# Point products of an FFT stage: three fp32r products from split operands in place of one float32 product

## The chip, the core and the metric

The kernel runs on one core of a Trainium2 chip. The metric is the device time of one execution in microseconds; the median of three executions is compared. The engines of a core work side by side: TensorE (PE in the profile; PEld is its weight load), VectorE (DVE), ScalarE (ACT), GpSimd (POOL) and SyncE (SP), the last of which here only issues DMA transfers.

## The reference

Three stages, eight batches of 3072 positions with 256 channels:

```python
X = np.fft.rfft(x, axis=1)
Y = X * (filt_r + 1j * filt_i)[None]
x = np.fft.irfft(Y, n=3072, axis=1).reshape(8 * 3072, 256)

h = np.maximum(np.maximum(x @ w1, x @ w2), x @ w3)       # d_ff 768
x = h @ w_out

h = x @ w_in                                             # d_ff 1024
e = np.exp(h - h.max(-1)); solu = h * e / (e.sum(-1) + 1e-9)
ln = (solu - mean) / sqrt(var + 1e-6) * g_ln
out = ln @ w_out
```

All data are float32 (the MoE weights float64, split in the kernel).

## The kernel before

Each of the sixteen channel halves ("channels" below, two for each batch, 128 columns wide) goes through an FFT of 3072 = 24 x 128 points, a product with the filter and the inverse FFT. The 24-point part is sums on VectorE (`dft8`, `fwd3` forward, `inv3`, `idft8` back). The 128-point part is a product with constant matrices on TensorE, the point product (`prod`, line 440), for four groups g of frequencies:

- `fwd_in` forms the twiddled input U (six blocks of 128 columns for groups 0 to 2, four for group 3) with two scalings on ScalarE and sums on VectorE.
- `middle` multiplies U by the matrices MA0 and MA1 into a PSUM tile pf, folds the result (Z), exchanges the partition halves of Z by DMA (`swap`), multiplies by the filter F (M1, M2), subtracts and adds on GpSimd, exchanges again, and forms EO with two operations on VectorE.
- `inv_out` multiplies EO by MB0 and MB1 into pf, and ScalarE and VectorE apply the inverse twiddles into the channel's slab S.

Channels 0 and 1 (`ch < FULL`) go the same way with full complex matrices (`dfull`) in `first_batch`, ahead of the first MoE. Channels 2 to 15 run as a stream of Python generators (`fft_stream`). The main loop traces one MoE step (`moe`: 12 products of `up`, 6 of `down`, in fp32r high and low terms), and then draws from the stream until a share of VectorE work (RATE, 3200 ns by the kernel's own costs) is spent, or nothing was spent in twelve draws. `later()` makes a generator yield until the next step has been traced; `behind_step()` orders VectorE's sums behind a MoE operation. A batch has 36 steps; the loop covers seven batches (`n_a`), and the last batch runs beside the weights of the second MoE. A channel can start when its slab is free (`free`), and its result must be there when `have` asks for it, one tile of the MoE ahead; the planner then puts the traced instructions of each engine in one fixed order.

Where a tile tag has one buffer, the next use waits for the last reader of the one before. Before the change U and EO have two buffers each (pool `f2`), M2 and the swap tile one (pool `fc`), and pf is one tile of two banks (`pairbank`) which the forward and the inverse products of all channels share. Products of float32 operands are issued as two instructions each; those of fp32r operands as one.

Of the kernel before, what the change touches and what calls it, by code (L numbers as in the profile page):

```python
# [20 lines left out]
P = 128  # L21
# [124 lines left out]
def kernel(ctx: ExitStack, tc: tile.TileContext, x0, xr, ff, tw, dft, first_f, first_i,  # L146
# [136 lines left out]

    FULL = 2

    cost = [0.0]

    def tt(o, a, b, op, eng=nc.vector):
# [146 lines left out]
        return t[:, j0:j1].rearrange("p s d -> p (s d)")  # L435

    def prod(o, mat, src, i0=None, i1=None, first=True, last=True):
        m = df[:, mat] if mat < 7 else dfull[:, mat - 7]
        v = src if i0 is None else rows(src, i0, i1)
        FZ['mm'] = nc.tensor.matmul(o, m, v, start=first, stop=last).ins  # L440

    def fwd_in(ch, g):
        sl, ks = GROUPS[g]
        X = S[ch]
        U = f2.tile([P, 8, P], F32, tag="U", name="U")
        n = len(ks)
        T = fc.tile([P, 6, P], F32, tag="T", name="T")
        if sl:
            for j, k in enumerate(ks):
                nc.scalar.activation(T[:, j:j + 4:3], X[:, sl:sl + 2, j], AF.Copy, scale=col("s", k))  # L450
                nc.scalar.activation(U[:, j:j + 4:3], X[:, sl:sl + 2, j], AF.Copy, scale=col("c", k))
            yield
            tt(U[:, 0:3], U[:, 0:3], T[:, 3:6], ALU.add)
            yield
            tt(U[:, 3:6], U[:, 3:6], T[:, 0:3], ALU.subtract)
            yield
        elif ch >= FULL:
            t, d = X[:, :, 1], X[:, :, 2]
            for j, k in enumerate((8, 20)):
                nc.scalar.activation(T[:, j], d[:, j], AF.Copy, scale=col("sh", k))  # L460
                nc.scalar.activation(U[:, j], t[:, j], AF.Copy, scale=col("c", k))
                nc.scalar.activation(T[:, 2 + j], d[:, j], AF.Copy, scale=col("ch", k))
                nc.scalar.activation(U[:, 2 + j], t[:, j], AF.Copy, scale=col("ns", k))
            yield
            tt(U[:, 0:4], U[:, 0:4], T[:, 0:4], ALU.add)
            yield
        else:
            t, d = X[:, :, 1], X[:, :, 2]
            nc.scalar.copy(U[:, 0], X[:, 0, 0])
            nc.scalar.activation(U[:, 1], X[:, 1, 0], AF.Copy, scale=col("c", 12))  # L470
            nc.scalar.activation(U[:, 5], X[:, 1, 0], AF.Copy, scale=col("ns", 12))
            nc.gpsimd.memset(U[:, 4], 0.0)
            yield
            for j, k in enumerate((8, 20)):
                nc.scalar.activation(T[:, j], d[:, j], AF.Copy, scale=col("sh", k))
                nc.scalar.activation(U[:, 2 + j], t[:, j], AF.Copy, scale=col("c", k))
                nc.scalar.activation(T[:, 2 + j], d[:, j], AF.Copy, scale=col("ch", k))
                nc.scalar.activation(U[:, 6 + j], t[:, j], AF.Copy, scale=col("ns", k))
            yield
            uu = U.rearrange("p (r s) d -> p r s d", r=2)[:, :, 2:4]  # L480
            tt(uu, uu, T[:, 0:4].rearrange("p (r s) d -> p r s d", r=2), ALU.add)
            yield
        ST["u", ch, g] = U
        yield

# [13 lines left out]
    def middle(ch, g):  # L499
        dc = ch % 2  # L500
        sl, ks = GROUPS[g]
        n = len(ks)
        W = n * P
        real = g == 3 and ch >= FULL
        R = 2 * P if real else 0
        foff = sum(2 * P * len(GROUPS[i][1]) for i in range(4 if real else g))

        def pair(tag, name, pool=fc):
            t = pool.tile([P, 2, 4, P], F32, tag=tag, name=name)
            return t.rearrange("p r s d -> p (r s d)")[:, :2 * W].rearrange("p (r w) -> p r w", r=2)  # L510

        def swap(v):

            t = fc.tile([P, 512], F32, tag="swap", name="swap")[:, :v.free_size()]
            nc.sync.dma_start(t[64:], v[:64])
            nc.sync.dma_start(t[:64], v[64:])
            return t

        odd = ch < 2 and UNITS.index((ch, g)) % 2
        F = pair("Z" if odd else "F", "F")  # L520
        nc.sync.dma_start(F.rearrange("p r w -> p (r w)"), ff[dc, :, foff:foff + 2 * W])
        src = ST.pop(("u", ch, g))
        pf = pairbank(ch)
        if ch < FULL:
            for r, (mr, mi) in enumerate(((FRR, FIR), (FRI, FII))):
                prod(pf[:, r, :W], mr, src, 0, n, True, False)
                prod(pf[:, r, :W], mi, src, n, 2 * n, False, True)
                yield
            M1 = pair("EO", "Y", f2)
            M2 = pair("M2" if odd else "M1", "M2")  # L530
            tt(M1, pf[:, 0:1, :W].to_broadcast([P, 2, W]), F, ALU.mult)
            yield
            tt(M2, pf[:, 1:2, :W].to_broadcast([P, 2, W]), F, ALU.mult)
            yield
            tt(M1[:, 0], M1[:, 0], M2[:, 1], ALU.subtract)
            SUMS[ch, g] = tt(M1[:, 1], M1[:, 1], M2[:, 0], ALU.add).ins
            yield
            ST["y", ch, g] = M1
            yield
            return  # L540
        u = col("u", 0)
        if real:
            prod(pf[:, 0, 0:P], MO, S[ch][:, 1, 0])
            prod(pf[:, 0, P:R], MF0, S[ch][:, 0, 0])
            prod(pf[:, 0, R:W], MA0, src, 0, 2)
            yield
            prod(pf[:, 1, R:W], MA1, src, 2, 4)
            TAKEN.add(ch)
        else:
            prod(pf[:, 0, :W], MA0, src, 0, n)  # L550
            yield
            prod(pf[:, 1, :W], MA1, src, n, 2 * n)
        yield
        Z = pair("Z", "Z")
        M2 = pair("M2", "M2")
        nc.scalar.mul(M2[:, 0, R:], pf[:, 1, R:W], -1.0)
        nc.scalar.copy(M2[:, 1, R:], pf[:, 0, R:W])
        if real:
            nc.scalar.copy(Z[:, 0, :R], pf[:, 0, :R])
        stt(Z[:, :, R:], pf[:, :, R:W], u, M2[:, :, R:])  # L560
        ZS = swap(Z[:, 0])
        yield
        M1 = pair("M1", "M1")
        tt(M1[:, :, R:], Z[:, 1:2, R:].to_broadcast([P, 2, W - R]), F[:, :, R:], ALU.mult)
        if real:
            tt(M1[:, 0, :R], Z[:, 0, :R], F[:, 0, :R], ALU.mult)
        yield
        EO = pair("EO", "EO", f2)
        tt(M2[:, :, R:], ZS[:, R:].unsqueeze(1).to_broadcast([P, 2, W - R]), F[:, :, R:], ALU.mult)
        if real:  # L570
            stt(M2[:, 1, :R], ZS[:, :R], col("sg", 0), F[:, 1, :R], ALU.mult)
        yield
        tt(M1[:, 1, R:], M1[:, 1, R:], M2[:, 0, R:], ALU.subtract, nc.gpsimd)
        RS = swap(M1[:, 1, R:])
        tt(M1[:, 0, R:], M1[:, 0, R:], M2[:, 1, R:], ALU.add, nc.gpsimd)
        if real:
            tt(EO[:, 0, :R], M1[:, 0, :R], M2[:, 1, :R], ALU.add, nc.gpsimd)
        yield
        yield from later()
        with behind_step():  # L580
            stt(EO[:, 0, R:], RS, u, M1[:, 0, R:], ALU.subtract)
            stt(EO[:, 1, R:], M1[:, 0, R:], u, RS)
        yield
        ST["y", ch, g] = EO
        yield

    def inv_out(ch, g):
# [3 lines left out]
        io = 0 if sl else 1  # L591
        src = ST.pop(("y", ch, g))
        pf = pairbank(ch)
        src = src.rearrange("p r (s d) -> p (r s) d", d=P)
        if ch < FULL:
            prod(pf[:, 0, :W], IRR, src, 0, n, True, False)
            prod(pf[:, 0, :W], IIR, src, n, 2 * n, False, True)
            yield
            prod(pf[:, 1, io * P:W], IRI, src, io, n, True, False)
            prod(pf[:, 1, io * P:W], III, src, n + io, 2 * n, False, True)  # L600
        elif not sl:
            prod(pf[:, 0, :P], MOI, src, 0, 1)
            prod(pf[:, 0, P:W], MB0, src, 1, n)
            yield
            prod(pf[:, 1, 2 * P:W], MB1, src, n + 2, 2 * n)
        else:
            prod(pf[:, 0, :W], MB0, src, 0, n)
            yield
            prod(pf[:, 1, io * P:W], MB1, src, n + io, 2 * n)
        yield  # L610

        def zz(r, j):
# [146 lines left out]
    def first_batch():  # L759
# [6 lines left out]
        xa = []  # L766
        for ch in range(2):
            xa.append(((fc if ch else yp).tile([P, 24, P], F32, tag=f"s{ch + 2}", name="xa"),
                       f2.tile([P, 8, P], F32, tag="EO", name="xq")))
            for q in range(4):  # L770
                nc.sync.dma_start(xa[ch][0][:NT, 8 * q:8 * q + 8] if q < 3 else xa[ch][1][:NT],
                                  x0[ch, :, 8 * q:8 * q + 8])
# [40 lines left out]
        for i, u in enumerate(UNITS):  # L813
# [28 lines left out]
            if i == 7:  # L842
                turn_in(0, 0, *UNITS[6])
        GATE.append(behind)
        with tc.issue_after(FZ["mm"]), tc.issue_after(FZ["sent"].ins):
            for q in range(4):
                quarter(3, q, nc.scalar, xs[3, q])
            busy(3)
# [477 lines left out]
```

## Time and profile before

| | |
|---|---|
| median of three executions | 2670.12 us (2669.33 to 2671.59) |
| profiled execution | 2671.45 us |
| its span, first to last instruction | 2669.7 us |
| TensorE busy | 2649.1 us (99%), granted clock 0.999 in the mean |
| weight loads busy | 2180.8 us (82%) |
| VectorE | 2114.0 us (79%) |
| ScalarE | 1559.3 us (58%) |
| GpSimd | 893.8 us (33%) |
| transfers from GpSimd's queue (the software ring) | 1296 packets, 4.72 MB |
| chain that ended last | 65% on TensorE, 2% of the span at the point products |

Busy times are the union of an engine's instructions. TensorE's instructions overlap, so the duration of one is longer than the distance from its start to the next start; when one is followed by another without a wait, that distance is its price. The FFT beside the first MoE lies between about 97 and 1340 us of the span, and the second MoE fills the rest from about 1600 us.

### The profile page before, as it was taken

What the parts mean: (1) busy time and instruction counts of PE and PEld (TensorE: products, weight loads), DVE (VectorE), ACT (ScalarE), POOL (GpSimd) and SP (SyncE); (2) the same over time, 40 slices, a digit from 0 to 9 for tenths busy, and PEclk for the clock granted to TensorE, in tenths of its full rate; (3) what the DMA queues carried; (4) which work ended last, traced back from release to release, by engine and by line L of the source; (5) the groups of instructions that cost most, each with busy time, mean ns of one, the idle gap of its engine ahead of it and who ended that gap; (6) DMA issues with size and microseconds to landing.
All of it is one profiled execution on the core that took longest, in us unless ns stands there. A gap on an engine that the chain in (4) does not pass through costs nothing.

```text
span 2669.7 us, 38591 instructions
## 1 busy us (share of the span) xinstructions
PE 2649.1 (99%) x12458; PEld 2180.8 (82%) x12458; DVE 2114.0 (79%) x3545; ACT 1559.3 (58%) x2960; POOL 893.8 (33%) x1311
## 2 busy tenths in 40 slices
PE   8999999999999999999999999999999999999999
PEld 5778888877887888888788888888888888888888
DVE  6887788988988988988785448878888878787875
ACT  5645554454454554554543336777777777777775
POOL 0011121011010010010110005666667676767675
PEclk9999999999999999999999999999999999999999
DMA  8534222224133242232222105555555555555543
GB/s 246 153 110 133 84 80 75 83 74 129 49 86 110 64 121 69 69 95 62 81 85 80 42 22 138 149 139 147 146 142 143 143 146 141 142 145 149 139 129 87
DMA packets 169063, 295.56 MB, mean 111 GB/s; under 512 B 33724, under 2 KB 101052, under 8 KB 167228
## 3 DMA queue, kind: packets, MB, share of 16 engines
q1 hardware_dynamic: 113848, 231.49, 32.4%
q10 hardware_dynamic: 53716, 56.89, 6.6%
q0 software_dynamic: 1296, 4.72, 0.6%
q8 instruction: 98, 1.61, 0.3%
q14 instruction: 105, 0.86, 0.1%
HBM read 97.40 MB, written 56.62 MB: 58 GB/s over the span
## 4 chain that ended last, share of the span: by engine, by line
PE 65%; DVE 2%; DMA 1%; SPq 1%; issue 1%; ACT 0%; POOL 0%; DVEq 0%; ACTq 0%; POOLq 0%
PE h L1112 20%; PE h L921 14%; PE p L1181 13%; PE p L1183 7%; PE o L942 2%; PE o L943 2%; PE o L941 2%; PE o L950 2%; PE pf L440 2%; SPq L881 1%; DMA raw<-in_w_out_dram 0%; DVE scr L291 0%; DMA raw<-in_w_in_dram 0%; DVE h L926 0%; DVE hl L930 0%
## 5 line engine op out<-in xcount | busy, mean ns | idle before, releaser
L291 POOL TENSOR_TENSOR M<-M,M 128x384 f32<-128x384 f32 (+1 forms) x112 | 129.8, 1179 | 1088.2 <-DVE M L291 921.2
L1174 POOL TENSOR_TENSOR sl<-zt,sh 128x1024 fp32r<-128x1024 f32 x188 | 453.4, 2412 | 120.9 <-ACT sh L1173 111.5
L929 ACT CAST hh<-h 128x512 fp32r<-128x512 f32 x288 | 169.3, 589 | 378.3 <-DVE h L926 369.2
L1181 PE MATMUL p<-V,sh 128*128 128x512 f32 x1536 | 380.4, 389 | 0.0
L1123 DVE SCALAR_TENSOR_TENSOR sp<-h,e 128x1024 f32<-128x1024 f32 x192 | 234.1, 1220 | 153.5 <-ACT e L1121 151.4
L1181 PEld LDWEIGHTS p<-V,sh 128*128 128x128 f32 x1536 | 287.3, 188 | 59.3
L1121 ACT ACTIVATE e<-h,sm 128x1024 f32<-128x1024 f32 x192 | 213.8, 1114 | 111.9 <-DVE sm L1119 68.3
L924 ACT ACTIVATE hm<-h 128x512 f32<-128x512 f32 x288 | 174.2, 606 | 170.5 <-PE h L921 169.5
L1119 DVE TENSOR_REDUCE sm<-h 128x1 f32<-128x1024 f32 x192 | 231.6, 1206 | 46.4 <-PE h L1112 45.3
L1173 ACT CAST sh<-zt 128x1024 fp32r<-128x1024 f32 x188 | 196.5, 1046 | 106.5 <-PE p L1181 92.6
L1125 ACT ACTIVATE e<-sp,sm 128x1024 f32<-128x1024 f32 x192 | 220.5, 1148 | 54.1 <-DVE sm L1127 46.8
L1112 PE MATMUL h<-wih,x2h 128*128 128x512 f32 x768 | 243.1, 392 | 1.2 <-ACT xo L953 1.2
L1112 PE MATMUL h<-wih,x2l 128*128 128x512 f32 x768 | 242.0, 391 | 0.0
L926 DVE TENSOR_TENSOR h<-hm,h 128x512 f32<-128x512 f32 x288 | 198.2, 690 | 51.2 <-PE h L921 46.8
L1112 PE MATMUL h<-wil,x2h 128*128 128x512 f32 x768 | 238.3, 390 | 0.0
L1140 DVE STREAM_TRANSPOSE yt<-sp 128x1024 f32<-128x1024 f32 x188 | 231.5, 1231 | 4.4 <-issue 0.5
L930 DVE TENSOR_TENSOR hl<-h,hh 128x512 fp32r<-128x512 f32 x288 | 197.2, 686 | 45.8 <-ACT hh L929 45.2
L941 PE MATMUL o<-hh,woh 128*128 128x512 f32 x576 | 232.6, 404 | 0.0
L942 PE MATMUL o<-hl,woh 128*128 128x512 f32 x576 | 228.1, 396 | 0.3 <-DVE hl L930 0.3
L943 PE MATMUL o<-hh,wol 128*128 128x512 f32 x576 | 225.8, 392 | 0.0
L1183 PEld LDWEIGHTS p<-V,sl 128*128 128x128 f32 x1536 | 209.7, 190 | 15.0
L1183 PE MATMUL p<-V,sl 128*128 128x256 f32 x1536 | 214.9, 282 | 0.0
(185 smaller groups left out, 5622.4 us busy)
## 6 DMA issues: line engine op xcount, KB each, us to landing
zt<-yt SPq DMA_DIRECT2D x752, 128.0 KB
x<-xo SPq DMA_DIRECT2D x96, 256.0 KB
x<-x ACTq DMA_DIRECT2D x48, 512.0 KB
F<-in_ff_dram SPq DMA_DIRECT2D x48, 384.0 KB
S<-in_xr_dram SPq DMA_DIRECT2D x12, 1536.0 KB
out_dram<-ob ACTq DMA_DIRECT2D x144, 128.0 KB
zt<-yt SPq DMA_DIRECT2D x560, 32.0 KB
F<-in_ff_dram SPq DMA_DIRECT2D x16, 512.0 KB
```

The costliest lines, as they stand in the source:

```text
L921: nc.tensor.matmul(ph[j], wt[:, c, f * P:(f + 1) * P], xt[:, c], start=i == 0, stop=i == 5)
L941: nc.tensor.matmul(po[m], wo_h[:, f, cs], hh, start=f == 0, stop=False)
L942: nc.tensor.matmul(po[m], wo_h[:, f, cs], hl, start=False, stop=False)
L943: nc.tensor.matmul(po[m], wo_l[:, f, cs], hh, start=False, stop=False)
L1112: nc.tensor.matmul(h[:, fs], xt[:, c, ts], wt[:, c, fs], start=n == 0, stop=n == 5)
L1119: nc.vector.tensor_reduce(sm[:, 0:1], h, axis=AX.X, op=ALU.max, negate=True)
L1123: nc.vector.scalar_tensor_tensor(sp, h, 1.0, e, op0=ALU.mult, op1=ALU.mult, accum_out=sm[:, 2:3])
L1125: nc.scalar.activation(e, sp, AF.Square, bias=sm[:, 3:4], accum_out=sm[:, 4:5])
L1140: nc.vector.transpose(out=YT[g][:, :, t].rearrange("p j c k -> p c j k"), in_=sp.rearrange("p (c j k) -> p c j k", c=NF2, j=4))
L1174: nc.gpsimd.tensor_tensor(lv, z, hv, op=ALU.subtract)
L1181: nc.tensor.matmul(p, sh[:, c], V2[:, c], start=c == 0, stop=False)
L1183: nc.tensor.matmul(p[:, :D], sl[:, c], V2[:, c, :D], start=False, stop=c == NF2 - 1)
```

## The change

- For channels 2 to 15 a new helper `split` rounds an operand to fp32r on ScalarE (hi) and subtracts hi from the operand on GpSimd (lo, also fp32r). `fwd_in` splits U of every group after its sums, `middle` splits EO of groups 0 to 2; both yield `later()` first, so the split is traced behind the next MoE step.
- `prod` with a split operand issues three fp32r products into the same PSUM range: high matrix with hi, low matrix with hi, high matrix with lo. The high and low matrices of MA0, MA1, MB0 and MB1 are formed once, after the first two channels, in the place of `dfull`. Group 3's EO and the two products MO and MF0 with slab columns stay float32.
- Buffers: U and EO have one buffer, with a hi tile and a lo tile beside it; the first two channels alternate between the operand's tile and the hi tile. M2 and the swap tile have two buffers. The inverse product of MB1 takes the whole width without `io`, which is 0 there.
- The scratch for dynamic DMA descriptors is set to 4096 bytes.

```diff
+    def split(v, tag, n):
+        hi = fc.tile([P, 8, P], F32R, tag=tag + "2", name=tag + "h")[:, :n]
+        lo = fc.tile([P, 6, P], F32R, tag=tag + "l", name=tag + "l")[:, :n]
+        nc.scalar.copy(hi, v)
+        nc.gpsimd.tensor_tensor(lo, v, hi, op=ALU.subtract)
+        return hi, lo
...
     def prod(o, mat, src, i0=None, i1=None, first=True, last=True):
+        if isinstance(src, tuple):
+            hi, lo = (rows(v, i0, i1) for v in src)
+            dh, dl = FZ["dh"][:, mat], FZ["dl"][:, mat]
+            nc.tensor.matmul(o, dh, hi, start=True, stop=False)
+            nc.tensor.matmul(o, dl, hi, start=False, stop=False)
+            nc.tensor.matmul(o, dh, lo, start=False, stop=True)
+            return
...
-        U = f2.tile([P, 8, P], F32, tag="U", name="U")
+        odd = ch < 2 and UNITS.index((ch, g)) % 2
+        U = fc.tile([P, 8, P], F32, tag="U2" if odd else "U", name="U")
...
+        if ch >= FULL:
+            yield from later()
+            U = split(U[:, :2 * n] if sl else U[:, :4], "U", 2 * n if sl else 4)
         ST["u", ch, g] = U
...
-            t = fc.tile([P, 512], F32, tag="swap", name="swap")[:, :v.free_size()]
+            t = f2.tile([P, 512], F32, tag="swap", name="swap")[:, :v.free_size()]
...
-            M1 = pair("EO", "Y", f2)
-            M2 = pair("M2" if odd else "M1", "M2")
+            M1 = pair("EO2" if odd else "EO", "Y")
+            M2 = pair("M2", "M2", f2)
...
-        M2 = pair("M2", "M2")
+        M2 = pair("M2", "M2", f2)
...
-        EO = pair("EO", "EO", f2)
+        EO = pair("EO", "EO")
...
+        if sl:
+            yield from later()
+            EO = split(EO.rearrange("p r (s d) -> p (r s) d", d=P), "EO", 6)
         ST["y", ch, g] = EO
...
-            prod(pf[:, 1, io * P:W], MB1, src, n + io, 2 * n)
+            prod(pf[:, 1, :W], MB1, src, n, 2 * n)
...
+        dd = fc.tile([P, 2, 4, P], F32R, tag="dfull", name="dd")
+        FZ["dh"], FZ["dl"] = dd[:, 0], dd[:, 1]
+        with tc.issue_after(FZ["sent"].ins):
+            nc.scalar.copy(FZ["dh"], df[:, 0:4])
+        nc.gpsimd.tensor_tensor(FZ["dl"], df[:, 0:4], FZ["dh"], op=ALU.subtract)
...
-    nc = bacc.Bacc("TRN2", target_bir_lowering=False, num_devices=1)
+    nc = bacc.Bacc("TRN2", target_bir_lowering=False, num_devices=1, dynamic_dma_scratch_size=4096)
```

## Rows read from the trace of the kernel before

**Rows 1.** Busy time by stretch: TensorE, weight loads, VectorE, ScalarE, GpSimd; clock, DMA.
```profile
97.00:1340.00 1243.00, 1239.00 (x5488) 999.05 (x5487) 1064.06 (x1639) 643.00 (x1462) 143.01 (x127) 1.00 0.30 88
```
**Rows 2.** Waits of TensorE, 97 to 1340 us: total, times, longest.
```profile
PE pf L440 <- POOL EO L291: 0.3, 1, 0.3
```
**Rows 3.** Order of time on TensorE, 1000.6 to 1002.7 us: start, duration, instructions.
```profile
1000.66 1.45 PE L440 MATMUL pf<-U,df 128*128 128x384 f32 x4
...
1002.18 0.63 PE L921 MATMUL h<-xh,w1h 128*128 128x512 f32 x2
```
**Rows 4.** Order of time on TensorE, 2000 to 2003 us, fp32r operands.
```profile
2000.19 1.98 PE L1181 MATMUL p<-V,sh 128*128 128x512 f32 x8
2002.01 1.12 PE L1183 MATMUL p<-V,sl 128*128 128x256 f32 x8
2002.96 0.40 PE L1112 MATMUL h<-wih,x2h 128*128 128x512 f32 x1
```
**Rows 5.** Order of time on TensorE, 1322 to 1324 us.
```profile
1322.43 1.03 PE L440 MATMUL pf<-U,df 128*128 128x256 f32 x4
...
1323.53 0.40 PE L942 MATMUL o<-hl,woh 128*128 128x512 f32 x1
```
**Rows 6.** Groups of TensorE by shape, point products: busy us, mean ns, idle before.
```profile
L440 PE MATMUL pf<-EO,df 128*128 128x384 f32 x196 | 72.6, 486 | 0.0
L440 PE MATMUL pf<-U,df 128*128 128x384 f32 x168 | 61.0, 485 | 0.0
...
L440 PE MATMUL pf<-U,df 128*128 128x256 f32 x56 | 14.4, 380 | 0.0
```
**Rows 7.** Groups by shape: a cast on ScalarE, a subtraction on GpSimd.
```profile
L1174 POOL TENSOR_TENSOR sl<-zt,sh 128x1024 fp32r<-128x1024 f32 x188 | 453.4, 2412 | 120.9 <-ACT sh L1173 111.5 <-PE p L1183 3.5 <-PE h L1112 2.4
...
L1173 ACT CAST sh<-zt 128x1024 fp32r<-128x1024 f32 x188 | 196.5, 1046 | 106.5 <-PE p L1181 92.6 <-POOL sm L1130 10.5 <-POOL sm L1131 2.1
```
**Rows 8.** Order of time on GpSimd, two places.
```profile
928.09 2.31 POOL L291 TENSOR_TENSOR M<-M,M 128x384 f32<-128x384 f32 x2 [11.94 <-DVE M L291]
...
1288.96 1.97 POOL L291 TENSOR_TENSOR M<-M,M 128x384 f32<-128x384 f32 x2 [66.17 <-ACT hm L924]
```
**Rows 9.** Order of time on VectorE, two places.
```profile
928.47 2.34 DVE L291 TENSOR_TENSOR S<-S,T 128x384 f32<-128x384 f32 x2
...
1319.20 1.02 DVE L291 TENSOR_TENSOR S<-S,T 128x384 f32<-128x384 f32 x2
```
**Rows 10.** Order of time on VectorE: the last sum of an operand.
```profile
511.49 1.02 DVE L291 TENSOR_TENSOR U<-U,T 128x384 f32<-128x384 f32 x2
...
1293.86 0.61 DVE L295 SCALAR_TENSOR_TENSOR EO<-M,tws,swap 128x384 f32<-128x384 f32 x1
...
1303.07 0.61 DVE L295 SCALAR_TENSOR_TENSOR EO<-M,tws,swap 128x384 f32<-128x384 f32 x1
```
**Rows 11.** Order of time on TensorE: the products of those operands.
```profile
513.04 1.45 PE L440 MATMUL pf<-U,df 128*128 128x384 f32 x4
...
1297.80 1.45 PE L440 MATMUL pf<-EO,df 128*128 128x384 f32 x4
...
1313.85 1.45 PE L440 MATMUL pf<-EO,df 128*128 128x384 f32 x4
```
**Rows 12.** Busy time by stretch of a pair (channels 13, 14), columns as rows 1.
```profile
1090.00:1163.00 73.00, 73.00 (x314) 58.20 (x313) 63.23 (x101) 43.08 (x104) 8.91 (x9) 1.00 0.29 79
1163.00:1229.00 66.00, 66.00 (x284) 52.60 (x283) 52.56 (x81) 31.09 (x71) 9.72 (x9) 1.00 0.37 106
1229.00:1281.00 52.00, 52.00 (x231) 43.07 (x230) 50.64 (x79) 25.55 (x55) 0.00 (x0) 1.00 0.14 40
```
**Rows 13.** Order of time on VectorE: the last operations of channel 15.
```profile
1358.52 1.82 DVE L295 SCALAR_TENSOR_TENSOR S<-scr 128x768 f32<-128x768 f32 x2
```
**Rows 14.** Order of time on TensorE: the first product of the last batch.
```profile
1430.05 0.62 PE L921 MATMUL h<-xh,w0h 128*128 128x512 f32 x2
```
**Rows 15.** The tile raws, 0 to 150 us: its transfers' time to landing.
```profile
DMA to landing us min/median/max: 4.1/4.9/11.2
```

More of the change, by code (lines that the diff above doesn't have):

```diff
@@ L593, in inv_out @@
         pf = pairbank(ch)
-        src = src.rearrange("p r (s d) -> p (r s) d", d=P)
+        if not isinstance(src, tuple):
+            src = src.rearrange("p r (s d) -> p (r s) d", d=P)
         if ch < FULL:
@@ L768, in first_batch @@
             xa.append(((fc if ch else yp).tile([P, 24, P], F32, tag=f"s{ch + 2}", name="xa"),
-                       f2.tile([P, 8, P], F32, tag="EO", name="xq")))
+                       fc.tile([P, 8, P], F32, tag="EO2" if ch else "EO", name="xq")))
             for q in range(4):
```

## The prediction

> **What bounds the kernel now.** I read the busy times first [rows 1]. From 97 us to 1340 us, where the FFT of channels 2 to 15 runs beside the first MoE, TensorE is busy for 1239.0 of 1243 us at a granted clock of 1.00, VectorE for 1064, ScalarE for 643, GpSimd for 143. So TensorE stands still for 4 us there, and the waits put 0.3 us of it at the point products, on the one operand that GpSimd makes today [rows 2]. This half is bound by TensorE's own work: a microsecond of it removed is a microsecond gained, unless a new wait takes its place. Behind 1340 us the change touches nothing, so all that it brings comes from the FFT half. The busy times of single groups overlap (a fp32r product shows 0.39 us and starts 0.23 us after the one before), so I take prices from starts alone.
>
> **The price of a float32 product.** A float32 product is issued as two instructions. In [rows 3] four of them (two products of 384 columns) start at 1000.66; with one fp32r product of 512 columns behind them they last until the next start at 1002.18. One fp32r product of 512 takes 0.2275 us: eight of them from 2000.19 to 2002.01 [rows 4]. So four instructions take 1.52 - 0.23 = 1.29 us, 0.322 each, 0.644 for a product. At 256 columns: 1322.43 to 1323.53 is 1.10 us [rows 5], less 0.23 is 0.87 for four, 0.435 for a product.
>
> **The price of its three fp32r products.** 256 columns: eight from 2002.01 to 2002.96 [rows 4], 0.119 each, three make 0.356. No row shows fp32r with 384 columns; its neighbours bound it, 0.119 (256) and 0.2275 (512), so three cost 0.356 to 0.683. The two prices lie on a line of 0.425 ns a column with 10 ns added, so I take 0.173, three 0.519. A product of 384 saves 0.644 - 0.519 = 0.125 us, one of 256 saves 0.435 - 0.356 = 0.079. The third weight load costs nothing: loads of 128 columns keep pace with products that start every 0.119 us too [rows 4].
>
> The Trainium skill, "TensorE: Matmul & The Clock Gate", Back-to-back issue gap, gives a sustained roofline of 81 ns a product at N=128 and 131 ns at N=512; an estimate between the two, about 114 ns at 384, would make three 0.34 us and the whole gain near 55 us. The trace differs: 227 ns at 512 in an unbroken stream, so the measurement decides.
>
> **How many.** [rows 6] count instructions, two a product. From U: 168 of 384 are 84 products, 56 of 256 are 28. From EO: 196 of 384 are 98, of which 14 (one a channel, group 3, which isn't split) stay, so 84. Together 168 products of 384 columns and 28 of 256: 168 x 0.125 = 21.0 us, and 28 x 0.079 = 2.2 us. The edit of the second inverse product changes nothing where sl is set (io is 0). TensorE loses 23.2 us of work. By the neighbours' prices for 384 columns it would be 4 us more work at one end and 50 us less at the other.
>
> **What is added.** Each of 14 channels gets seven splits (four U, three EO), 98 in all, 84 of 768 elements and 14 of 512. ScalarE's rounding: a cast of 1024 elements takes 1046 ns [rows 7], so some 0.78 us for 768 and 0.52 for 512, 73 us in all. ScalarE has 600 us free [rows 1]: that costs only latency. GpSimd's subtraction: 2412 ns for 1024 [rows 7], so 1.81 and 1.21 us, 84 x 1.81 + 14 x 1.21 = 169 us, on an engine with 1100 us free. Its 143 us become about 312.
>
> What isn't free is that GpSimd and VectorE stop each other. Two subtractions on GpSimd take 1.97 us in one place and 2.31 in another [rows 8]; beside the second, two sums of 384 on VectorE take 2.34 us, where the same two take 1.02 with GpSimd idle [rows 9]. For VectorE I bound the loss by nothing (the undisturbed pair) and by all of GpSimd's new 169 us; nearest is the disturbed pair, 1.3 us lost beside 2.31, about half. Since a good part of VectorE's instructions read PSUM or find GpSimd done, I take 0.5 us a split, 49 us. VectorE then has 1113 of some 1220 us, 91%: still not the bound as a mean.
>
> The Trainium skill, "SBUF — State Buffer", SBUF: two separate sides, says why: the port pair is an exclusive lock, and a VectorE operation with two SBUF inputs and a GpSimd operation block each other for the whole instruction. The stretched pair agrees. [...]
>
> **Low terms that come late.** A product now waits for a cast and a subtraction, 2.6 us and two handovers, and TensorE is in order: an operand that isn't there stops all MoE products behind it. Today's room from operand to product: in channel 7, which starts alone, U of group 0 is done at 512.51 and used at 513.04; in channel 15 EO of group 0 is done at 1294.47 and used at 1297.80, EO of group 1 at 1303.68 and 1313.85 [rows 10, 11]. So the later groups have the room, the first EO has part of it, the first U of a channel that starts alone has none. The order is fixed when the kernel is built, with the new operations in it, and the operand that GpSimd makes today cost TensorE 0.3 us in 14 uses [rows 2]. Bounds: nothing, and 98 x 2.6 = 255 us if every product stood for the whole of it. Near the lower end: I take 0.3 us for each of the 14 first EO, 4.2 us, and nothing for the rest. The gating by one step costs nothing by itself: the product moves behind the next step's 18 products, and TensorE has those to do.
>
> **The chain of channels.** The FFT is a chain of its own: a pair of channels takes 73 us for the groups of the odd one, 66 for the even one, 52 for an inverse and a forward transform with VectorE at 97% [rows 12]. It must give the last batch its input. VectorE's last operation for channel 15 ends at 1360.3 [rows 13]; the last batch's first product is at 1430.05 [rows 14]. Between them must lie two transposes, an exchange by DMA, two casts and two differences, by my estimate 12 us (4.9 for a transfer as in [rows 15], the rest at about 1 us each), so 58 us of margin; the MoE that now runs 20 us earlier leaves 38. What the change adds to the chain, in a pair: 14 x 0.5 us of lost VectorE time, half of it hidden in idle time (10 and 13 us in the two group stretches), 3.5; some 3 us of latency at each of two first EO and one first U, 9; less 16 uses of the point products' PSUM tile that are 0.25 us shorter, 4; less some 2 us as M2 and the swap tile no longer wait. That is 6.5 us, about 39 in six pairs: just about the margin. Bounds: nothing, and by the whole of the lost time and latency 6 x 23 - 38 = 100 us. I take nothing.
>
> **The start.** The constants' rounding and subtraction (0.5 and 1.2 us) stand once, ahead of the first split, on engines that are mostly free. With a smaller ring a weight transfer on GpSimd's queue could wait for the one ahead, at most the 4.9 us that a transfer takes [rows 15]; its weights serve later columns of the first tile: I take nothing. U, EO and M2 of the first two channels alternate between two tiles as they did.
>
> **Sum.** The profiled execution took 2671.45 us, its span 2669.7 and 1.75 around it; it is 1.3 above the median of 2670.12. 2671.45 - 23.2 + 4.2 = 2652.4; against the median 2651.
>
> **Rivals.** *The chain ends late (slower).* If the chain grows by 12 us a pair (0.9 us lost a split with half of it hidden, 6; 9 of latency; less half of the 6 that come back), it is 72 us, 34 past the margin: TensorE stands before the last batch, 2651 + 34 = 2685. It costs from 6.3 us a pair on and eats the whole gain at about 9.5. For it: VectorE at 97% in the inverse and forward stretch can't catch up, and the 2.34 us pair. Against: GpSimd stands still in just that stretch [rows 12]. *TensorE waits for the low terms.* At 0.2 us for each of 98 splits, 19.6 us, the sum is 2670.1 - 23.2 + 19.6 = 2666.5, no change to speak of. For it: subtractions stretch beside VectorE. Against: the room of the later groups. *The fp32r products of 384 columns cost as much as those of 512.* Then 168 products cost 0.039 us more each: 2670.1 + 6.6 - 2.2 + 4.2 = 2679. Against it: 256 and 512 scale. *A price below the line.* With 0.119 us at 384 the 168 products save 48 us: 2670.1 - 48.4 - 2.2 + 4.2 = 2624. Against: the same two rows.
>
> **Numbers.** The forecast has 0.58, the late chain 0.20, the waits for low terms 0.15, products that save nothing 0.04, the price below the line 0.03. No change is within 0.2%, 5.3 us, about what a measurement here can tell. Faster: 0.58 + 0.03 and a third of the waits, 0.66; within: half of the waits and the edges of the late chain, 0.13; slower: 0.21. The likeliest case alone: 2643 to 2661. The range: 2643 (23.2 us and the 4 us of standing gone) to 2680 (up to the middle of the late chain).
>
> **What would show it.** TensorE's starts: three products of 384 in 0.52 us. TensorE's waits on GpSimd's low terms at the point products: about 4 us. Between the end of channel 15 and the last batch's first product: more than 12 us, and no gap in TensorE there. VectorE's sums of 384 beside GpSimd: longer than 0.65 us in the mean. The prediction is wrong if TensorE's standing time ahead of the last batch grows by more than 10 us, or if fp32r at 384 isn't near 0.173 us.

## The result and the profile after

The changed kernel takes 2705.65 us (2699.53 to 2707.99, four runs) where the kernel before takes 2669.90; the ratio is 1.0122, interval 1.0102 to 1.0142. It is 1.2% slower. The forecast was 2651 us, the range ended at 2680: direction and range are both wrong. Of the rivals, the late chain of channels has the right sign, with a price too small and, as the lines below show, only part of the cause.

The page of the changed kernel, its line of busy times and its line of the granted clock (the profiled execution took 2707.99 us):

```profile
span 2706.2 us, 39180 instructions
...
PE 2647.7 (98%) x12654; PEld 2214.1 (82%) x12654; DVE 2158.3 (80%) x3545; ACT 1627.7 (60%) x3059; POOL 1084.4 (40%) x1410
...
PEclk9999999999999999998999999999999999999999
```
The cores' view of the same run, span and mean granted clock:

```profile
core 0: 2706.2 us, clock 0.991
```
These lines split the loss. Before, TensorE was busy for 2649.1 of 2669.7 us at a mean clock of 0.999. Standing time is span less busy time: 20.6 before, 58.5 after, **+37.9 us**. What a lower clock costs is estimated as (1 - mean clock) x span: 2.7 before, 24.4 after, **+21.7 us**. Busy time less that is work at full clock: 2646.4 before, 2623.3 after, **-23.1 us**. Together +36.5 us, the difference of the spans. (The third decimal of the clock is worth 1.3 us either way. The estimate also counts time at the lower clock in which TensorE stands; that it isn't far off is shown by e18 below, which has the same products at a clock of 0.999 and 2621.4 us of work.) So TensorE's work fell as forecast; standing and clock took it back two and a half times over.

Busy time by stretch, columns as in [rows 1]: 97 to 1040 us in the kernel before; then in the changed one the same stretch, the FFT half, and one bad stretch in it.

```profile
97.00:1040.00 943.00, 939.00 (x4193) 757.04 (x4192) 805.39 (x1244) 490.46 (x1120) 114.98 (x100) 1.00 0.31 94
```
```profile
97.00:1040.00 943.00, 921.71 (x4290) 770.54 (x4289) 798.37 (x1177) 522.00 (x1135) 233.83 (x162) 0.99 0.30 89
...
97.00:1340.00 1243.00, 1201.50 (x5520) 1001.58 (x5519) 1056.45 (x1563) 679.98 (x1485) 304.23 (x209) 0.98 0.28 85
...
1225.00:1290.00 65.00, 48.84 (x206) 39.88 (x205) 51.37 (x76) 34.94 (x80) 19.91 (x14) 0.85 0.23 64
```
Where [rows 1] had 4 us of standing there are now 41.5: 21.3 up to 1040 us (4.0 before) and 20.2 from there on (none before). From 1225 to 1290 TensorE stands for 16 us, 7.8 of them in one piece, and the granted clock is 0.85: with 1.0 for 2.4 GHz and 0.5 for 1.2, that is 30% of the stretch at the lower level.

The waits of TensorE in the changed kernel, total, times, longest; below them VectorE's `hl` in the kernel before.

```profile
PE o L970 <- DVE hl L958: 14.5, 11, 2.9
PE pf L449 <- ACT EOh L290: 7.8, 1, 7.8
...
PE o L969 <- ACT hh L957: 6.0, 3, 2.5
PE h L949 <- ACT hm L952: 5.1, 5, 2.0
PE pf L449 <- DVE Z L303: 3.2, 2, 2.2
PE pf L449 <- ACT S L674: 2.4, 1, 2.4
...
PE pf L451 <- POOL EOl L291: 1.7, 1, 1.7
```
```profile
PE h L921 <- DVE hl L930: 1.4, 1, 1.4
...
PE o L942 <- DVE hl L930: 0.3, 2, 0.2
```
The larger part of the growth, some 22 us, isn't at the point products: `hl`, `hh` and `hm` are the MoE's own steps on VectorE and ScalarE. One place where they are late, in order of time on VectorE, and below it GpSimd and TensorE:

```profile
631.03 0.68 DVE L958 TENSOR_TENSOR hl<-h,hh 128x512 fp32r<-128x512 f32 x1
631.63 2.88 DVE L299 TENSOR_TENSOR scr<-scr 128x384 f32<-128x384 f32 x2
634.43 2.63 DVE L299 TENSOR_TENSOR S<-scr 128x768 f32<-128x768 f32 x2
...
639.65 0.68 DVE L958 TENSOR_TENSOR hl<-h,hh 128x512 fp32r<-128x512 f32 x1
```
```profile
630.69 2.10 POOL L291 TENSOR_TENSOR Ul<-U,Uh 128x768 fp32r<-128x768 f32 x1 [9.95 <-DMA zt<-yt]
632.76 2.62 POOL L299 TENSOR_TENSOR M<-M,M 128x384 f32<-128x384 f32 x2
```
```profile
640.38 0.80 PE L970 MATMUL o<-hl,woh 128*128 128x512 f32 x1 [2.87 <-DVE hl L958]
```
Two pairs of sums take 2.88 and 2.63 us beside a subtraction and GpSimd's two older operations. Undisturbed, a pair of 384 takes 1.02 [rows 9] and a pair of 768 takes 1.82 (as in VectorE's row at 1451.26 below). The next `hl` waits behind them, and TensorE stands for 2.87 us. The Trainium skill, "SBUF — State Buffer", SBUF: two separate sides, gives the exclusive lock on the shared port pair as the reason; the stretched pairs agree.

Most of the rest lies at one place. In order of time on TensorE, the end of the sixth batch and the start of the seventh, and VectorE's last operation for the seventh batch's input (channel 13):

```profile
1265.71 0.61 PE L978 MATMUL o<-xh,al 128*128 128x512 f32 x2
1274.10 0.69 PE L449 MATMUL pf<-EOh,dd 128*128 128x384 f32 x1 [7.77 <-ACT EOh L290]
...
1276.76 0.69 PE L451 MATMUL pf<-EOl,dd 128*128 128x384 f32 x1 [1.65 <-POOL EOl L291]
1277.24 0.52 PE L449 MATMUL pf<-EOh,dd 128*128 128x384 f32 x1
1277.56 0.52 PE L450 MATMUL pf<-EOh,dd 128*128 128x384 f32 x1
...
1287.37 0.63 PE L949 MATMUL h<-xh,w0h 128*128 128x512 f32 x1
```
```profile
1267.84 2.70 DVE L303 SCALAR_TENSOR_TENSOR S<-scr 128x768 f32<-128x768 f32 x2
```
From 1266 to 1287 us TensorE has no MoE product: the seventh batch's input is done in the slab at 1270.5 and reaches the first product at 1287.4. Between them stand 18 point products of the next channels, and TensorE waits 14.0 us for them (7.8 and 1.7 on the split EO, 2.4 on S, 2.2 on Z). In the kernel before, 69 us lay between the end of channel 13 and that product; here it is 16.8. The point products now start 0.32 us apart, where they take 0.175 at the full clock (below). By an estimate from the starts (18 point products with 0.147 us more each, and nine MoE products behind them at 0.43 us instead of 0.2275) the lower clock costs 4 to 5 us here.

The chain of channels, which the prediction let end at about 1399 us: VectorE's last operation for channel 15, the issue of the exchange behind it, and TensorE's first product of the last batch ([rows 13, 14] answer).

```profile
1451.26 1.82 DVE L303 SCALAR_TENSOR_TENSOR S<-scr 128x768 f32<-128x768 f32 x2
```
```profile
1454.92 10.12 SPq L909 DMA_DIRECT2D zt<-yt  x16
```
```profile
1471.09 0.39 PE L949 MATMUL h<-xh,w0h 128*128 128x512 f32 x1
```
It ends at 1453.1, 92.8 us later than before, and only 18 us lie between it and the last batch's first product, where 70 lay. The margin is gone. But TensorE hardly stands there; its row ahead of the last batch has 2.7 us of standing:

```profile
1433.00:1475.00 42.00, 39.27 (x165) 31.72 (x164) 35.53 (x59) 18.15 (x38) 5.06 (x4) 0.96 0.28 90
```

### The profile page after: what moved, and what is told of

Same layout as the page of the kernel before. It is cut to its first block, busy times and chain, and to the rows that moved or that the text cites. A ratio compares the mean times of both kernels' runs of the same rounds, so it can differ in the third digit from the quotient of the medians.

```text
span 2706.2 us, 39180 instructions
## 1 busy us (share of the span) xinstructions
PE 2647.7 (98%) x12654; PEld 2214.1 (82%) x12654; DVE 2158.3 (80%) x3545; ACT 1627.7 (60%) x3059; POOL 1084.4 (40%) x1410
## 4 chain that ended last, share of the span: by engine, by line
PE 64%; DVE 7%; issue 2%; DMA 1%; SPq 1%; ACT 1%; POOL 1%; DVEq 0%; ACTq 0%; POOLq 0%
PE h L1140 19%; PE h L949 14%; PE p L1209 13%; PE p L1211 7%; PE o L970 2%; PE o L971 2%; PE o L969 2%; PE o L978 2%; DVE scr L299 1%; SPq L909 1%; DVE S L299 1%; DVE h L954 1%; DVE M L299 1%; DMA swap<-M 1%; DVE S L303 1%
## 5 line engine op out<-in xcount | busy, mean ns | idle before, releaser
L291 POOL TENSOR_TENSOR Ul<-U,Uh 128x768 fp32r<-128x768 f32 (+1 forms) x56 | 114.5, 2045 | 571.3 <-ACT Uh L290 513.8
L954 DVE TENSOR_TENSOR h<-hm,h 128x512 f32<-128x512 f32 x288 | 197.4, 686 | 66.4 <-PE h L949 56.7
```

The source lines that it names most:

```text
L954: nc.vector.tensor_tensor(ph[1], hm, ph[1], op=ALU.max)
```

## The experiments

Each kernel below was measured beside the kernel before on the same chip; the latter took 2670 to 2674 us each time. All values are from the profiled execution but the first two columns; standing, clock and work are worked out as above, "end" is the end of the last VectorE operation for channel 15. e1, e2, e4 and e18 leave the low term out of the result (the third product reads the high term or the whole operand again): they price parts and are no versions to use.

| run | median us | ratio (interval) | standing | clock | work | end |
|---|---|---|---|---|---|---|
| before | 2669.9 | | 20.6 | 2.7 | 2646.4 | 1360 |
| after | 2705.65 | 1.0122 (1.0102 to 1.0142) | 58.5 | 24.4 | 2623.3 | 1453 |
| e1_no_subtraction | 2667.59 | 0.9977 (0.9968 to 0.9987) | 35.1 | 8.0 | 2623.4 | 1409 |
| e2_subtraction_unread | 2703.29 | 1.0114 (1.0099 to 1.0129) | 56.7 | 13.5 | 2631.3 | 1427 |
| e7_subtraction_vector | 2695.61 | 1.0083 (1.0068 to 1.0098) | 51.0 | 24.2 | 2618.5 | 1442 |
| e8_halved_subtraction | 2715.15 | 1.0165 (1.0147 to 1.0182) | 60.6 | 21.7 | 2627.3 | 1459 |
| e3_no_gate | 2720.77 | 1.0176 (1.0159 to 1.0193) | 65.8 | 29.9 | 2623.7 | 1464 |
| e4_no_cast | 2651.12 | 0.9920 (0.9905 to 0.9934) | 24.2 | 2.6 | 2622.2 | 1368 |
| e18_cast_two_buffers | 2651.31 | 0.9923 (0.9905 to 0.9941) | 25.0 | 2.6 | 2621.4 | 1372 |
| e6_buffers_only | 2682.14 | 1.0049 (1.0033 to 1.0064) | 26.5 | 2.7 | 2647.9 | 1359 |
| e14_scratch_only | 2671.74 | 1.0001 (0.9992 to 1.0011) | 19.1 | 2.7 | 2648.4 | 1360 |
| e15_tiles_scratch8 | 2680.96 | 1.0035 (1.0021 to 1.0048) | 25.7 | 5.4 | 2647.8 | 1362 |
| e9_u_only | 2688.50 | 1.0061 (1.0046 to 1.0076) | 40.3 | 8.1 | 2637.5 | 1412 |
| e10_eo_only | 2674.92 | 1.0008 (0.9999 to 1.0017) | 28.3 | 8.0 | 2638.0 | 1394 |
| e13_late_groups | 2682.32 | 1.0043 (1.0029 to 1.0057) | 35.8 | 2.7 | 2640.0 | 1411 |
| e11_eo_late | 2668.64 | 0.9990 (0.9981 to 0.9999) | 24.9 | 2.7 | 2640.4 | 1353 |
| e12_eo_late_vector | 2667.14 | 0.9986 (0.9977 to 0.9995) | 22.1 | 5.3 | 2642.0 | 1365 |
| e16_eo_late_single | 2671.01 | 0.9999 (0.9990 to 1.0008) | 25.3 | 0.0 | 2643.9 | 1371 |
| e17_eo_late_vector_single | 2668.16 | 0.9990 (0.9981 to 0.9999) | 24.5 | 5.3 | 2640.5 | 1382 |
| e19_eo_late_two_buffers | 2667.91 | 0.9990 (0.9981 to 0.9999) | 24.4 | 5.3 | 2641.7 | 1367 |

### Is it the subtraction?

**Left out (e1):**
```diff
-        lo = fc.tile([P, 6, P], F32R, tag=tag + "l", name=tag + "l")[:, :n]
...
-        nc.gpsimd.tensor_tensor(lo, v, hi, op=ALU.subtract)
-        return hi, lo
+        return hi, hi
```


> Of the change, GpSimd's subtraction is left out: the third product reads the high term again, so the result lacks the low term; casts, gating, buffers and the number of products stay. Theory A (GpSimd's 98 subtractions and VectorE's sums block each other, which makes MoE operations and the chain of channels late): most of the loss goes, 2650 to 2665 us, and TensorE's short standing times between 300 and 1200 us (15 us in the changed kernel) fall below 4. Theory B (latency of cast, gating and one-buffer operands in the chain, not the blocking): part of the latency stays, 2680 to 2700 us. Theory C (three fp32r products aren't cheaper): no gain over 2670 whatever else happens.

**Made and not read (e2):** `return hi, hi` alone.

> The subtraction stays on GpSimd, but its result is read by no product (the third product reads the high term again, so the result lacks the low term). Theory A (blocking): the blocking is all there, so the time stays within 12 us of the changed kernel, 2694 to 2712 us. Theory B (latency of the low term ahead of the products): the product needs the cast alone, so it falls by half of the loss or more, to 2660 to 2690 us. Difference to the run without subtraction: under A 30 us or more, under B less than 10.

**On VectorE (e7):** `nc.vector.tensor_tensor(lo, v, hi, ...)`.

> The 98 subtractions run on VectorE in place of GpSimd: no blocking by them, but VectorE gets 84 x 0.95 + 14 x 0.68 = 89 us of work, more than the 44 us that it lost in the changed kernel by longer sums. Theory A in its strong form (blocking hurts because it comes between operations with a fixed order, VectorE's load itself doesn't): faster than the changed kernel, 2665 to 2690 us. If VectorE's total load is what makes the chain late: 2700 to 2730 us.

**In two halves (e8):**
```diff
-        nc.gpsimd.tensor_tensor(lo, v, hi, op=ALU.subtract)
+        for j in range(2):
+            h = slice(j * n // 2, (j + 1) * n // 2)
+            nc.gpsimd.tensor_tensor(lo[:, h], v[:, h], hi[:, h], op=ALU.subtract)
```


> Each subtraction on GpSimd is issued as two of half the length; nothing else changes. If what costs is the sum of GpSimd's time (theory 1): 2703 to 2712 us, as the change or a little more. If it is the length of one instruction, behind which a VectorE operation has to stand (theory 2): 2680 to 2698 us, with fewer operations of VectorE at over 2.5 us.

Without the subtraction 38 us come back (by the table 23 of standing and 16 of clock); made but unread it costs as much as ever, within the noise. So it isn't TensorE waiting for the low term, it is that the subtraction runs. Halving it makes it worse by 9.5 us (5.8 when each is taken against the kernel before that was measured beside it). So shorter instructions are no remedy here; what the length alone costs the run doesn't say, since GpSimd's busy time also grows by 30 us. On VectorE it is cheaper by 10 us, though VectorE's own busy time is then the highest of all (2193.5 us).

VectorE's product of 768 elements, grouped by shape over 97 to 1470 us, in the kernels before, after and e1: busy us, mean ns, idle before.

```profile
L291 DVE TENSOR_TENSOR M<-swap,F 128x768 f32<-128x768 f32 x42 | 40.0, 954 | 11.7 <-DMA swap<-Z 11.7
```
```profile
L299 DVE TENSOR_TENSOR M<-swap,F 128x768 f32<-128x768 f32 x42 | 49.0, 1168 | 8.4 <-DMA swap<-Z 8.2
```
```profile
L297 DVE TENSOR_TENSOR M<-swap,F 128x768 f32<-128x768 f32 x42 | 39.8, 948 | 8.1 <-DMA swap<-Z 7.8
```
954 becomes 1168 ns and falls back to 948 when GpSimd no longer subtracts. There is a second cost, in the waits of ScalarE over the same stretch of the changed kernel:

```profile
ACT U L477 <- POOL Ul L291: 18.8, 10, 3.7
ACT U L467 <- POOL Ul L291: 18.3, 20, 1.9
```
For 37 us ScalarE can't write the next group's U, because there is one U tile now and the subtraction still reads it; the MoE's `hm` and `hh` are queued behind. On VectorE (e7) this wait is 26 us, in halves (e8) 49. How the 38 us divide between the two costs stays open: the full split with two U tiles wasn't tried.

**The step behind the sums (e3):** both new `yield from later()` taken out.

> Both new yields to the next step are left out; the splits follow their sums at once, everything else as in the change. If the gating makes the chain late (theory B's part): 2670 to 2690 us. If the blocking does (theory A): within 10 us of 2705, since the subtractions are the same and as long.

15 us slower than the change: the step that the operands wait in the order is a help, not the cause.

Some of these times fit none of the ranges expected. e1 lies between those of its theories A and B, and TensorE's standing between 300 and 1200 us fell to 9.6 us, not below 4; so the blocking isn't the whole loss. e3 and e8 are slower than either theory had it, and e7 lies between its two, so neither the order of the operations nor VectorE's load alone sets its time.

### What is left without the subtraction

e1 saves the same 23 us of work as the forecast and keeps only 4. Two runs ask where the rest is.

**No cast either, two tiles (e4):** U and EO are fp32r tiles that VectorE writes, and `split` returns its operand twice.
```diff
...
-        U = fc.tile([P, 8, P], F32, tag="U2" if odd else "U", name="U")
+        U = f2.tile([P, 8, P], F32R if ch >= FULL else F32, tag="U", name="U")
...
-        EO = pair("EO", "EO")
+        EO = pair("EO", "EO", f2, F32R if sl else F32)
```


> VectorE writes the point products' operands straight as fp32r; there is no cast and no subtraction, U and EO have two buffers again, and the third product reads the same operand as the first (the low term is left out of the result). The new steps of the order stay. Run without the subtraction alone the kernel took 2667.6 us, 17 us more than the 23 us of saved TensorE work would leave of 2671. Theory 1, the rest is the latency of the casts and the single buffers in the chain of channels: 2647 to 2655 us, channel 15 done near 1370 us. Theory 2, the rest is the two steps that the operands now wait in the order: 2662 to 2668 us, channel 15 done after 1400 us.

**Casts, two tiles (e18):** e1 with the lines below; the first two channels' tiles follow, and the high tile has six blocks.
```diff
-        U = fc.tile([P, 8, P], F32, tag="U2" if odd else "U", name="U")
+        U = f2.tile([P, 8, P], F32, tag="U", name="U")
...
-        EO = pair("EO", "EO")
+        EO = pair("EO", "EO", f2)
```


> ScalarE's 98 casts stay and the subtraction is left out, as in the run without the subtraction (2667.6 us), but U and EO have two buffers as before; the third product reads the rounded operand again (the low term is left out of the result). Theory 1, the rest of 16 us between that run and the one without casts (2651.1) is the casts, their latency in the chain and their time on ScalarE ahead of the MoE: 2663 to 2668 us. Theory 2, it is the single buffers, for which a channel's next group waits: 2650 to 2656 us.

Both take the forecast's 2651 us. The casts cost nothing; the 16 us are the single U and EO tiles. The last VectorE operation of channel 15 in e1 and in e18:

```profile
1406.93 1.82 DVE L301 SCALAR_TENSOR_TENSOR S<-scr 128x768 f32<-128x768 f32 x2
```
```profile
1369.85 1.82 DVE L301 SCALAR_TENSOR_TENSOR S<-scr 128x768 f32<-128x768 f32 x2
```
One tile instead of two lengthens the chain by 37 us. Theory 1 of e18, the casts, is out. Which of the two tiles costs how much with all splits was not tried.

### The double tiles and the scratch

**Both, products float32 (e6):** of the change only `f2` for M2 and `swap`, the first channels' M2, and the scratch of 4 KB.

> Only the double M2 and exchange tiles and the DMA scratch of 4 KB; all point products float32, no split, no new step, U and EO with two buffers. Theory 1, the whole effect of the change is in products and splits: 2668 to 2674 us, no change. Theory 2, the buffers take waits out of the chain of channels or the small scratch delays transfers: more than 5 us off either way.

**The scratch alone (e14):**

> The kernel before with the DMA scratch of 4 KB alone. The run with scratch and double tiles took 11.6 us more than before with no product changed. Theory 1, the smaller scratch holds transfers back: 2678 to 2684 us. Theory 2, the double tiles shift the order: 2668 to 2673 us.

**The tiles with a scratch of 8 KB (e15):**

> Double M2 and exchange tiles as in the change, first channels included, with a DMA scratch of 8 KB instead of 4; float32 products. Theory 1 (the scratch): between 2668 and 2676 us, less than with 4 KB. Theory 2 (the tiles): 2678 to 2685 us, as with 4 KB.

The scratch costs nothing. The double tiles cost the float32 kernel 10 to 12 us: they don't shorten the chain (1359 and 1362), and TensorE stands 5 to 6 us more, at other places in a changed order. The longest of them in e6, which before doesn't have, is a product of U that waits 2.4 us until ScalarE has read the products' PSUM tile for the inverse transform. e6's profiled execution is the shortest of its four runs, 3 us under their median, so not all of the cost is seen in it. e4 and e18 have the double tiles too and reach the forecast, so this cost doesn't simply add to that of the splits.

### Fewer splits

**U alone (e9), EO alone (e10):** the other operand stays float32 with two tiles.

> Only U is split, 56 of the 98 splits; EO stays float32 with its two buffers. TensorE saves 12.7 us of work. If each split costs the same (theory 1: the 36 us that the subtractions cost and the 17 us of the rest, by 56/98, are 30 us): 2685 to 2692 us. If the first part of the delay is eaten by the margin that the chain of channels had before the last batch (theory 2): 2660 to 2675 us.

> Only EO is split, 42 of the 98 splits; U stays float32 with its two buffers. TensorE saves 10.5 us of work. Theory 1, each split costs the same (53 us by 42/98 are 23 us): 2680 to 2687 us. Theory 2, the margin eats the first part: 2658 to 2670 us.

**Groups 1 and 2 of both (e13), of EO (e11):**
```diff
-        if sl:
+        if g in (1, 2):
             yield from later()
             EO = split(EO.rearrange("p r (s d) -> p (r s) d", d=P), "EO", 6)
```


> U and EO are split in groups 1 and 2 alone, 56 of the 98 splits, all of 768 elements; groups 0 and 3 stay float32. TensorE saves 14 us of work. Theory 1, each split costs the same (0.55 us for one of U as with U alone, 0.35 for one of EO): 25 us, 2680 to 2685 us. Theory 2, the splits at the start of a channel cost, where there is no room: 2658 to 2668 us.

> EO is split in groups 1 and 2 alone, 28 of the 98 splits; group 0, the first of each channel, stays float32, and so does U. TensorE saves 7.0 us of work. Theory 1, each split of EO costs what it did with all 42 (14.5 us of cost, 0.35 us each, 9.7 us here): 2671 to 2676 us. Theory 2, what cost was TensorE standing for the low term of the first group, and the lower granted clock behind it: 2662 to 2667 us, with no wait of TensorE for a low term.

U costs more than EO: against 2669.9 us and the 2673.6 measured beside them, 56 splits of U lose 15 to 19 us, 42 of EO 1 to 5. The costliest wait of TensorE in e9 and that for the low terms in e10:

```profile
PE h L946 <- ACT hm L949: 12.7, 6, 4.3
```
```profile
PE pf L451 <- POOL EOl L291: 4.9, 2, 2.8
```
With U it is ScalarE's part of the MoE that is late, behind the 40 us for which ScalarE waits on the single U tile there. With EO it is the low term of a channel's first group, in two places (near 817 and 1217 us), and the granted clock is 0.93 in the 25 us around each. e11 leaves that group out and has neither; it gains 0.1%. e13 shows that U costs in its later groups too: 14 us lost against e11, with 28 more splits.

**EO's groups 1 and 2 alone, as e11, with the low term on VectorE (e12), with single M2 and exchange tiles and 12 KB of scratch (e16 on GpSimd, e17 on VectorE), and as e12 with two EO tiles (e19):**

> As the run with EO split in groups 1 and 2 alone, but the 28 subtractions are on VectorE. With all 98 splits this place was 10 us cheaper than GpSimd. Theory 1, what costs is GpSimd's hold of VectorE: 1 to 4 us less than on GpSimd, 2661 to 2668 us. Theory 2, VectorE's own time counts as much: the same as on GpSimd within 2 us.

> EO split in groups 1 and 2 alone, subtraction on GpSimd, but M2 and the exchange tile single as before and the DMA scratch at 12 KB. With the double tiles and 4 KB this took 2668.6. If what the buffers alone cost (11.6 us) was in that time too: 2656 to 2662 us. If the cost of the buffers shows only where the products are float32: 2665 to 2670 us.

> As the run before, with the 28 subtractions on VectorE. With the double tiles and 4 KB this took 2667.1. If the cost of the buffers was in that time: 2655 to 2661 us; if not: 2664 to 2669 us.

> EO split in groups 1 and 2 alone (28 splits), subtraction on VectorE, double M2 and exchange tiles, and EO again with two buffers; U float32 with two. With a single EO tile this took 2667.1 us. TensorE saves 7.0 us of work. Theory 1, the single EO tile held the chain here too: 2660 to 2664 us. Theory 2, with no split at the start of a channel the single tile had cost nothing: 2665 to 2669 us.

All lie between 2667 and 2671 us. e12 has the lowest median of the versions with both terms: 0.14% under the kernel before (0.05 to 0.23), 38 us under the changed one; e11, e17 and e19 can't be told from it. None gets the 7 us of its saved work. The single EO tile costs nothing here (e12 and e19). e10, e11 and e16 lie outside the ranges of both their theories, by 1 to 5 us.

## Why the prediction was wrong

**The price of the products was right.** Two float32 products of 384 columns are now six fp32r ones; in order of time on TensorE, the first of six and the instruction behind them:

```profile
1380.05 0.34 PE L449 MATMUL pf<-Uh,dd 128*128 128x384 f32 x1
...
1381.10 0.40 PE L978 MATMUL o<-xl,ah 128*128 128x512 f32 x1
```
1.05 us for six, 0.175 each (0.173 taken). Work fell by 23.1 us (23.2 taken; so close a match is luck, as the third decimal of the clock alone is worth 1.3 us), and by the same in e1, e3, e4 and e18 within 2 us; in e2, e7 and e8 it is up to 8 us off, which I can't explain. The rivals of a dearer or a cheaper product are out. So is the estimate of 0.114 us that the prediction worked out from the Trainium skill, "TensorE: Matmul & The Clock Gate", Back-to-back issue gap: the trace has 0.175.

**Low terms that come late: right for the subtraction, short for the cast.** The term of 4.2 us was for a product that waits for a cast and a subtraction. On the low terms TensorE waited 1.7 us, on the rounded EO 7.8 more, in one place, where EO itself came late in the chain ahead of the seventh batch. e2, whose products don't wait for the low terms, gains 2.4 us, which is not clear of noise.

**VectorE's lost time: right in size, wrong in what it does.** 0.5 us a split made 49 us; VectorE's busy time grew by 44.3 (2114.0 to 2158.3). The step laid it all on the chain of channels, and put nothing on the MoE's own steps. TensorE stood 15.0 us for `hl` against 1.7 before, and with `hh` and `hm` 26 against 4. Of the 37.9 us, 17.3 came before 1040 us. Of the batches that start there, the fourth and the fifth have their input done 64 and 38 us ahead of their first product, and TensorE doesn't stand right ahead of it: there a late chain isn't the reason. This is a step of the prediction that failed: "a microsecond of it removed is a microsecond gained, unless a new wait takes its place", and the new wait had no term.

**The chain of channels: the other step that failed.** It took 6.5 us a pair, 39 over six, "just about the margin", and so nothing. The chain grew by 92.8 us, 15.5 a pair. The ends in the table divide this, with the parts taken out in this order: 44 with the subtractions (1453 to 1409, e1), 37 with the single U and EO tiles (1409 to 1372, e18), 4 with the casts (to 1368, e4), 8 with what is left of the change. For the splits the step took 21 us of lost VectorE time and 54 of latency, 75; with subtractions and casts it is 48. What failed are other terms. The 36 us that it gave back for shorter products and a second M2 and exchange tile didn't come: what is left of the change is 8 us longer, not 36 shorter, and e6, which has these tiles alone, ends where the kernel before ends. The single tiles had no term: the step costed the tiles that M2 and the exchange gain, not those that U and EO lose in channels 2 to 15. And the 12 us from the chain's end to the first product were too few: the exchange is 16 transfers, whose issue alone took 10.1 us, and in the five kernels whose chain used the room up (the changed one, e1, e3, e7, e8) 14.7 to 18.0 us are left there.

**Where the late chain stopped TensorE.** The prediction's sign of being wrong was standing ahead of the last batch, more than 10 us of it. There it was 2.7; ahead of the seventh batch it was 14.0, by the same mechanism one batch sooner. The prediction's own rule, chain less 38 us of margin, gives 2651 + 92.8 - 38 = 2706 with the measured growth, which is the time after; it also comes near e7 (81 us, 2694), e8 (99, 2712), e3 (104, 2717), e4 and e18 (8 and 12, within the margin, 2651), and is 6 us short for e1 (48, 2661). This agreement shows less than it seems to: the rule puts 55 us of standing ahead of the last batch, and the trace has 2.7 there. Where the room is used up, the last batch starts 15 to 18 us behind the chain's end, wherever TensorE has stood. The rule doesn't fit e2 (67, 2680 for 2703), where 33 us still lie between the chain's end and the last batch and TensorE stands as long all the same, nor e9 and e13. So both are there in the changed kernel, late MoE steps and a late chain; how much of one is brought on by the other the runs don't show.

**The clock: a term that was missing.** Standing was costed one for one. It cost 37.9 us and the lower level of the clock some 21.7 more by the estimate, over half as much again. In e4 and e18, where TensorE stands for 24 and 25 us, the clock stays at 0.999. In e2 it stands for 56.7 us, spread over the FFT half, and the estimate is 13.5; in e7 for 51.0, of which 14.8 lie between 1040 and 1100 us and 11.7 between 1225 and 1290, at 0.83 and 0.87, and the estimate is 24.2.

**The rivals.** The late chain is borne out in part: it stopped TensorE, ahead of the seventh batch and not of the last, and its price (12 us a pair, 2685) was too low; nor does it account for the standing before 1040 us, as far as the fourth and the fifth batch show. Its upper bound, 23 a pair, was on record and kept out of the range; from the terms given, 14 x 0.5 and 9, the whole is 16 a pair, so that the 23 can't be worked out again.

## What to carry to other kernels

When a change makes room by taking second tiles away, price each tile that is lost as a new wait, and name what is queued behind the engine that will wait; here that was 16 us without any added arithmetic. Before work goes to a free engine, ask whom it holds up: 191 us more of busy GpSimd cost 38 us on a kernel that TensorE bounds, and under 2 of them at the product that reads the result. The cost of GpSimd includes the U tile that the subtraction holds. And price standing of TensorE above one for one, above all where much of it falls within some tens of microseconds.

## What the runs showed of the hardware

- GpSimd's subtraction of 768 elements takes 1.8 us by scale from its 1024; in place the mean was 2.30 (U) and 2.05 us (EO), the shortest 1.83 and 1.81 and the longest 4.84 and 4.23. Beside VectorE it is held up as well. The groups by shape of the changed kernel, 97 to 1470 us:

```profile
L291 POOL TENSOR_TENSOR Ul<-U,Uh 128x768 fp32r<-128x768 f32 x42 | 96.4, 2296 | 540.7 <-ACT Uh L290 483.1 <-DVE scr L299 16.1 <-PE o L978 15.1
...
L291 POOL TENSOR_TENSOR EOl<-EO,EOh 128x768 fp32r<-128x768 f32 x42 | 85.9, 2046 | 217.1 <-ACT EOh L290 199.3 <-DVE S L299 9.6 <-issue 5.8
```
- The same subtraction on VectorE (e7) took 1.02 and 0.97 us.
- 16 us of standing out of 65, in pieces of 7.8 us and less, went with a granted clock of 0.85 between 1225 and 1290 us; the kernel before kept 1.00 through its FFT half. From 480 to 1040 us, 12.3 us of standing out of 560 in the changed kernel went with 0.99.
- The exchange of a tile by 16 transfers from one queue took 10.1 us to issue, and 16.8 and 18.0 us lay between the end of a channel and the first product that reads it, ahead of the seventh and the last batch of the changed kernel.
